# Even frequencies through both transforms first, batch 1's scans behind them

## The chip, the cores and the metric

The kernel runs on one core of a Trainium2 chip. The metric is device time of one execution in microseconds. Three runs of the kernel before gave 487.95, 489.83 and 489.97 us; the median is 489.83 us. The engines are named as the profile names them: PE (TensorE, matmul), DVE (VectorE), ACT (ScalarE), POOL (GpSimd) and SP (SyncE, whose queue issues most transfers here).

## The reference

Three blocks run one after the other on a batch of 2, 768 tokens and 8 heads of 48 (so 384 model columns):

```python
# 1. attention with a decaying state, per batch and head
y[t] = r[t] @ (state + (u * k[t])[:, None] * v[t])      # u: the token's own term
state = w[t][:, None] * state + k[t][:, None] * v[t]
# 2. Fourier mixing over tokens and columns, then a wide layer
mixed = real(fft(fft(x, axis=1), axis=2)); u = x + mixed
un = (u - mean(u)) / sqrt(var(u) + 1e-6)                # over the 384 columns
x = u + relu(un @ w_ch1) @ w_ch2                        # 384 -> 1536 -> 384
# 3. gated layer with a spatial product over the 768 tokens
h = gelu_tanh(x @ w_in); a, v = h[..., :512], h[..., 512:]
out = x + (a * (w_sg @ (norm(v) * g) + b_sg)) @ w_out
```

## The kernel before, in words

**Attention** (`attention`, line 345) goes by head pairs: n = 0 to 3 are the pairs of batch 0, n = 4 to 7 those of batch 1. Tokens stand in 6 chunks of 128. `prep` (line 191) loads the pair's decays `wx`, its r and k (`rk`) and v, and on DVE makes the running product of the decays (L224, "the scan"), then L236, L240 and L241 scale r and k by it; ACT does logarithm and exponential (L229, L230), POOL one product (L238). PE then multiplies scores (`sc_ps`, L281), transposes k (`kn_ps`, L295), makes chunk states (`kv_ps`, L304; chained by a scan on DVE, L310; copied by ACT, L312) and values (`y_ps`, L324 and L333). L335 adds the token's own term, L340 and L341 sum and subtract token halves, and ACT (L342) and POOL or DVE (L343) write the result as a high and a low part, `AH` and `AL`. The tiles P, rk, prk, XE, XO are the places of decays and r, k; pairs 1, 2 and 3 use `prk`, `XE` and `XO`.

**The own term** (`own_term`, line 249) has two forms. For the pairs in the set `TM` (4 to 7 before) `prep` loads r, k and u in token order (`in_ruk`, L215), and it is two elementwise products (L255 on DVE or POOL by the set `PV`, L257 on POOL) and a sum on DVE (L258). For the others DVE multiplies r and k (L234) and PE sums over head columns with six matmuls (`dg_ps`, L264), which ACT copies (L265). Either way POOL multiplies the sum by v (L270).

**The Fourier step** (`fourier`, line 451) has `frequencies` (the transform over tokens for one third j of the columns, on PE into `x_ps`, high part by ACT L400 and low part by DVE L401), `own_tokens` (PE brings x itself into the right layout, `t_ps`, copied by ACT L420 into `uT`) and `mixed` (the transform over columns, `d_ps`, added to `uT` by DVE, L440 to L449). Frequencies with even and odd index (e = 0 and 1) are apart: e = 0 gives the first half of the columns of `uT`, e = 1 the second.

**The wide layer** (`moe1`, line 460) goes over four halves of 384 tokens: (batch 0, e = 0), (batch 0, e = 1), and the same of batch 1. Each half is centred (`centre`: the mean by matmuls `mu`, then `uc`, L488; `split_centred`: `us`, L494 and L495), then for 12 blocks f of hidden columns PE makes `z_ps` (9 matmuls), ACT the high part (L518), DVE the low part `z_lo` (L519), and PE `ch` (9 matmuls, one block behind). Every weight block is read as 8-byte words and turned into a high and low part: three operations on DVE (L162 to L164, into the one buffer `st`), one on ACT (L168), one on POOL (L169).

**Order.** The code is written as generators that are stepped in turn, and a scheduler then orders each engine's queue; every queue runs in that order. Before, attention of batch 1 is stepped beside the Fourier step of batch 0 (`merge` with `F0`, line 884), and the rest of it, with batch 1's Fourier step, beside the wide layer (`merge(first(), second(), FR)`, line 914). A second set of rules are order-only dependencies (`behind`). The last stage (`gating`) follows when the wide layer is done; the change does not touch it.

Of the kernel before, what the change touches and what calls it, by code (L numbers as in the profile page):

```python
# [20 lines left out]

FR = 0.7
CFG1 = dict(v=2, dv=2, dg=2, sc=4, yt=2)
CFGF = dict(ps=2, su=2)
F0 = 1.0
KC = 9
LA = 6
KV = range(1)
NJ0 = 28
JP = -1000000  # L30
LNPE = ((0, 0), (0, 1))
GF = 4
STB = 1
TB = 1
XB = 1
LEAD = 0
PV = range(4)
TM = range(4, 8)
YB = 1
# [7 lines left out]
C = 128  # L47
# [48 lines left out]
def fused(ctx, tc, ins, out, dbg=None):  # L96
# [94 lines left out]
    def prep(n, b, p, ap):  # L191
# [6 lines left out]
        v = m1.tile([C, NC_ * 2 * D], F32, name="v", tag=("us_hi", "us_lo")[p - 2]) if b == 0 and p >= 2 else ap([C, NC_ * 2 * D], "v")  # L198
        if b == 0 and p < 3:
            prod, y0 = (x[:PR, p * S:(p + 1) * S].rearrange("p (c t) -> p c t", c=NC_) for x in spare)  # L200
        else:
            prod = ap([C, ROW], "prod") if n in TM else ap([PR, NC_, C], "prod")
            y0 = ap([PR, NC_, C], "y0")

# [11 lines left out]
        for c0, c1 in parts:  # L216
# [9 lines left out]
            if b:  # L226
                behind(scan, summed[min(n - 2, NP - 1)])
            Pi = P[:, cs, 1:C + 1]
# [162 lines left out]

    def frequencies(b, AB, X, j):

        for e in range(2):
            nx = NCOS[e] + NSIN
            x_ps = ps(b, [C, 512], "x_ps", XB)[:, :nx]
            for c in range(3):
                mm3(x_ps, AB[:, 3 * e + c, j * C:(j + 1) * C], tdft[:, e, c, :nx], c == 0, c == 2)
            x = X[e][j][:, :nx]
            nc.scalar.copy(x.hi, x_ps)  # L400
            nc.vector.tensor_tensor(out=x.lo, in0=x_ps, in1=x.hi.bitcast(F32), op=ALU.subtract)  # L401
            yield
# [20 lines left out]
    def mixed(b, ap, X, uT, e):  # L423
# [18 lines left out]
        for f, (d, s) in enumerate(us):  # L442
            for g, x, y in ((0, d, s),) if f == 0 else ((1, d, s), (2, s, d)):
                ut = uT[:, g, e * HT:(e + 1) * HT]

                to, x = ut[:, :HT // 2 + 1 - e], x[:, :HT // 2 + 1 - e]
                nc.vector.tensor_tensor(out=to, in0=to, in1=x, op=ALU.add)
                to, y = ut[:, HT // 2 + 1 - e:][:, ::-1], y[:, 1 - e:HT // 2]
                nc.vector.tensor_tensor(out=to, in0=to, in1=y, op=ALU.add)  # L449

    def fourier(b, ap, back, AB, X, uT, js):
        for j in js:
            yield from frequencies(b, AB, X, j)
        yield from own_tokens(b, back, AB, uT)
        for e in range(2):
            mixed(b, ap, X, uT, e)
            yield


    def moe1(mp, halves, uT, w1, w2):  # L460
# [69 lines left out]

        ucs = centre(*halves[0])
        last = None
        for n, (b, h) in enumerate(halves):
            us = split_centred(ucs)
            sq = ucs[0]
# [293 lines left out]
    with ExitStack() as main, ExitStack() as low, ExitStack() as late, ExitStack() as att:  # L829
# [26 lines left out]
        def through(b, p):  # L856

            if b == 0 and p > 0:
# [200 lines left out]
```

## Time and profile before

| | us |
|---|---|
| median of three runs | 489.83 |
| the profiled execution | 486.78 |
| its span, first to last instruction | 485.0 |
| PE busy / DVE / ACT / POOL in the span | 433.7 / 269.1 / 173.1 / 177.1 |

The span is what the views below divide; the profiled execution lasts 1.8 us longer than its span and 3.05 us less than the median of the runs. "Busy" counts the time in which an engine has an instruction under way; PE's matmuls overlap each other, so their durations add up to more than their busy time. PEclk is the clock that was granted to PE as a share of full speed, and 1.00 is full speed. In the timeline a row reads: start, duration of the run of equal instructions, engine, line, operation, what it writes from what, shapes, count, and in brackets how long the engine had stood idle before it and what ended that.

### The profile page before, as it was taken

How to read it: one execution, taken by the hardware profiler on the slowest of the kernel's cores; microseconds unless marked ns; L12 is line 12 of the kernel's file. 1: busy time of each engine (PE TensorE's matmuls, PEld its weight loads, DVE VectorE, ACT ScalarE, POOL GpSimd, SP SyncE). 2: the span in 40 equal slices, each digit the busy share in tenths (PEclk: the TensorE clock that was granted, in tenths of full speed). 3: DMA queues.
4: the chain of work that ended last, by engine and by line, in shares of the span. 5: the costliest groups of instructions: out<-in, count | busy, mean ns of one | idle time of the engine just before them, and what ended most of it. 6: DMA issues, size and time to landing. Idle time of an engine off the chain costs nothing. (4 is left out here: it accounts for less than half of the span.)

```text
span 485.0 us, 6874 instructions
## 1 busy us (share of the span) xinstructions
PE 433.7 (89%) x2666; PEld 409.1 (84%) x2666; DVE 269.1 (55%) x453; ACT 173.1 (36%) x368; POOL 177.1 (37%) x179
## 2 busy tenths in 40 slices
PE   9569973896896968999999799999999999999995
PEld 9468863885796957999999599999988998999994
DVE  5983259967697686463137961452148734811332
ACT  3534453552452433443323531431355403311110
POOL 2864366754466463320003540110356524200330
PEclk9869997698997987999999999999999999999998
DMA  8983504341644311040000310000243200010002
GB/s 209 266 303 82 164 1 148 118 133 55 257 146 132 106 38 33 1 131 0 1 0 2 109 55 0 1 0 1 65 115 84 64 1 2 33 66 1 0 18 88
DMA packets 14074, 36.75 MB, mean 76 GB/s; under 512 B 1808, under 2 KB 5680, under 8 KB 13648
## 3 DMA queue, kind: packets, MB, share of 16 engines
q1 hardware_dynamic: 13456, 32.54, 22.3%
q0 software_dynamic: 576, 3.68, 2.2%
q8 instruction: 23, 0.38, 0.3%
q14 instruction: 19, 0.16, 0.1%
HBM read 33.86 MB, written 2.36 MB: 75 GB/s over the span
## 5 line engine op out<-in xcount | busy, mean ns | idle before, releaser
L109 PE MATMUL ch<-z_hi,w 128*128 128x384 f32 x288 | 82.1, 343 | 5.7 <-ACT z_hi L518 2.9
L109 PE MATMUL z_ps<-us_hi,w 128*128 128x384 f32 x288 | 83.1, 351 | 1.4 <-ACT us_hi L494 1.4
L519 DVE SCALAR_TENSOR_TENSOR z_lo<-z_ps,z_hi 128x384 fp32r<-128x384 f32 x48 | 26.5, 553 | 68.9 <-ACT z_hi L518 68.2
L109 PEld LDWEIGHTS ch<-z_hi,w 128*128 128x128 f32 x288 | 53.1, 191 | 8.2 <-ACT z_hi L518 4.4
L109 PEld LDWEIGHTS z_ps<-us_hi,w 128*128 128x128 f32 x288 | 54.3, 193 | 3.6 <-ACT us_hi L494 2.0
L109 PE MATMUL ch<-z_lo,w 128*128 128x384 f32 x144 | 50.3, 350 | 5.7 <-DVE z_lo L519 5.5
L109 PE MATMUL z_ps<-us_lo,w 128*128 128x384 f32 x144 | 49.6, 344 | 0.0
L518 ACT ACTIVATE z_hi<-z_ps 128x384 fp32r<-128x384 f32 x48 | 23.3, 489 | 55.0 <-PE z_ps L109 41.4
L285 POOL TENSOR_SCALAR_AFFINE_SELECT sc<-sc 128x384 f32<-128x384 f32 x32 | 23.9, 769 | 41.2 <-ACT sc L284 41.2
L608 POOL TENSOR_TENSOR vn_lo<-t_g,vn_hi 128x384 fp32r<-128x384 f32 x16 | 16.1, 1014 | 57.1 <-ACT vn_hi L607 57.1
L109 PEld LDWEIGHTS ch<-z_lo,w 128*128 128x128 f32 x144 | 27.8, 193 | 7.6 <-DVE z_lo L519 7.4
L604 DVE SCALAR_TENSOR_TENSOR t_g<-s_ps,g,bsg 128x384 f32<-128x384 f32 x16 | 9.6, 616 | 43.2 <-PE s_ps L109 43.0
L169 POOL TENSOR_TENSOR w<-st,w 128x384 fp32r<-128x384 f32 (+1 forms) x18 | 24.8, 1380 | 22.9 <-ACT w L168 22.8
L109 PE MATMUL s_ps<-wsg_hi,vn_lo 128*128 128x384 f32 x96 | 32.3, 336 | 0.0
L109 PE MATMUL s_ps<-wsg_hi,vn_hi 128*128 128x384 f32 x96 | 32.3, 336 | 0.0
L109 PE MATMUL s_ps<-wsg_lo,vn_hi 128*128 128x384 f32 x96 | 32.3, 336 | 0.0
L333 PE MATMUL y_ps<-v,sc 128*128 128x120 f32 (+1 forms) x192 | 31.6, 287 | 0.0
L109 PEld LDWEIGHTS z_ps<-us_lo,w 128*128 128x128 f32 x144 | 27.9, 194 | 0.1
L333 PEld LDWEIGHTS y_ps<-v,sc 128*128 128x128 f32 x192 | 26.7, 197 | 0.8 <-issue 0.5
L169 POOL TENSOR_TENSOR win_lo<-st,win_hi 128x384 fp32r<-128x384 f32 x8 | 8.3, 1053 | 48.8 <-ACT win_hi L168 48.8
L169 POOL TENSOR_TENSOR wsg_lo<-raw,wsg_hi 128x384 fp32r<-128x384 f32 x12 | 12.4, 1035 | 32.3 <-ACT wsg_hi L168 32.2
L109 PE MATMUL x_ps<-tdft,AH 128*128 128x386 f32 (+1 forms) x72 | 20.3, 374 | 4.2 <-ACT AH L342 4.2
(261 smaller groups left out, 1047.5 us busy)
## 6 DMA issues: line engine op xcount, KB each, us to landing
raw<-in_w SPq DMA_DIRECT2D x12, 384.0 KB, 3.9
w_raw<-in_w SPq DMA_DIRECT2D x12, 384.0 KB, 4.6
raw<-in_win SPq DMA_DIRECT2D x8, 384.0 KB, 3.6
prod<-in_ruk SPq DMA_DIRECT2D x4, 624.0 KB, 4.3
tdft<-in_tdft POOLq DMA_DIRECT2D x2, 1158.0 KB, 9.2
v<-in_v SPq DMA_DIRECT2D x8, 288.0 KB, 6.0
raw<-in_wsg SPq DMA_DIRECT2D x12, 192.0 KB, 2.4
out<-o SPq DMA_DIRECT2D x12, 192.0 KB, 1.9
```

Source lines behind the costliest of these rows:

```text
L109: nc.tensor.matmul(o, lhsT=x, rhs=y, start=start and i == 0, stop=stop and i == len(ps) - 1, **kw)
L169: nc.gpsimd.tensor_tensor(out=w.lo[to], in0=x, in1=w.hi[to].bitcast(F32), op=ALU.subtract)
L285: nc.gpsimd.affine_select(out=sc, in_=sc, pattern=[[0, 3], [1, C]], compare_op=ALU.is_gt, fill=0.0, base=0, channel_multiplier=-1)
L333: nc.tensor.matmul(y3[:, i, to], lhsT=sc[h][:, i, :], rhs=vf[:, of], start=c == 0, stop=True, skip_group_check=c > 0)
L518: nc.scalar.activation(out=z.hi, in_=z_ps, func=AF.Relu)
L519: nc.vector.scalar_tensor_tensor(out=z.lo, in0=z_ps, scalar=0.0, in1=z.hi.bitcast(F32), op0=ALU.max, op1=ALU.subtract)
L604: nc.vector.scalar_tensor_tensor(out=t, in0=s_ps[h], scalar=g[:, f:f + 1], in1=bsg[:, hs], op0=ALU.mult, op1=ALU.add)
L608: nc.gpsimd.tensor_tensor(out=vn.lo[:, f, 3 * h:3 * h + 3], in0=th, in1=vn.hi[:, f, 3 * h:3 * h + 3].bitcast(F32), op=ALU.subtract)
```

## The change

Four things change. The own terms of pairs 1, 2 and 3 take the elementwise form (`TM` from 1), so their `in_ruk` loads, 624 KB each, come between the first loads. Attention of batch 1 is no longer stepped beside batch 0's Fourier step; its scans stand behind the last addition of that step's even frequencies (`first_through`, order only). The Fourier step does e = 0 through `frequencies`, `own_tokens` and `mixed` before it does e = 1, and the first half is centred in between. The first two weight blocks are stepped earlier, four rather than six blocks are kept ahead (`GF`, `LA`), `FR` goes from 0.7 to 0.6, so each step of the wide layer takes 1.67 rather than 1.43 steps of batch 1 with it, and the second half's mean is made as the others (two additions on DVE, a split on ACT and POOL, two matmuls) instead of three matmuls in f32.

```diff
-FR = 0.7
+FR = 0.6
-F0 = 1.0
-LA = 6
+LA = 4
-LNPE = ((0, 0), (0, 1))
-GF = 4
+LNPE = ((0, 0),)
+GF = 2
-TM = range(4, 8)
+TM = range(1, 8)
...
             if b:
-                behind(scan, summed[min(n - 2, NP - 1)])
+                behind(scan, first_through)
...
-    def frequencies(b, AB, X, j):
-
-        for e in range(2):
+    def frequencies(b, AB, X, j, *es):
+
+        for e in es:
...
     def fourier(b, ap, back, AB, X, uT, js):
         for j in js:
-            yield from frequencies(b, AB, X, j)
+            yield from frequencies(b, AB, X, j, 0)
         yield from own_tokens(b, back, AB, uT)
-        for e in range(2):
-            mixed(b, ap, X, uT, e)
-            yield
+        end = mixed(b, ap, X, uT, 0)
+        yield end
+        for j in js:
+            yield from frequencies(b, AB, X, j, 1)
+        mixed(b, ap, X, uT, 1)
+        yield
...
         ucs = centre(*halves[0])
+        us = split_centred(ucs)
+        yield 0, -1
...
-        merge(fourier(0, f_room, ..., uT[0], (2,)), att_steps, F0, False, LEAD)
+        for got in fourier(0, f_room, ..., uT[0], (2,)):
+            if got:
+                first_through = got
+                mixing = moe1(m1, HALVES, uT, w1, w2)
+                next(mixing)
...
-        ahead(GF)
-        mixing = moe1(m1, HALVES, uT, w1, w2)
         merge(first(), second(), FR)
```

Where instructions stand now is shown at three places of DVE's queue. First the opening, where the pairs of batch 0 are prepared. Before (AH and prod take r times k, prk is pair 1, XE pair 2, XO pair 3):

```order
L234 TENSOR_TENSOR AH<-prk 112x768
L241 SCALAR_TENSOR_TENSOR rk<-AL,rk 112x384
L656 TENSOR_TENSOR unit<-unit 112x1
L236 SCALAR_TENSOR_TENSOR prk<-prk 112x768
L224 SCALAR_TENSOR_TENSOR XE<-XE,d_91 112x774
L234 TENSOR_TENSOR AH<-XE 112x768
L240 SCALAR_TENSOR_TENSOR AL,unit<-prk,AL 112x768
L236 SCALAR_TENSOR_TENSOR XE<-XE 112x768
L224 SCALAR_TENSOR_TENSOR XO<-XO,d_91 112x774
L241 SCALAR_TENSOR_TENSOR prk<-AL,prk 112x768
L310 SCALAR_TENSOR_TENSOR kn<-kn,dec 112x288
```

In the changed kernel, at the same place:

```order
L236 SCALAR_TENSOR_TENSOR prk<-prk 112x768
L241 SCALAR_TENSOR_TENSOR rk<-AL,rk 112x384
L662 TENSOR_TENSOR unit<-unit 112x1
L255 TENSOR_TENSOR AH<-AH 128x576
L224 SCALAR_TENSOR_TENSOR XE<-XE,d_91 112x774
L240 SCALAR_TENSOR_TENSOR AL,unit<-prk,AL 112x768
L241 SCALAR_TENSOR_TENSOR prk<-AL,prk 112x768
L236 SCALAR_TENSOR_TENSOR XE<-XE 112x768
L310 SCALAR_TENSOR_TENSOR kn<-kn,dec 112x288
L258 TENSOR_REDUCE dg<-AH 128x12
L224 SCALAR_TENSOR_TENSOR XO<-XO,d_91 112x774
```

L241 of pair 1 (`prk`) stood behind the scans of XE and XO and two products L234; now it stands behind the scan of XE and the product L255.

Next the end of batch 0's attention. Before, from the last subtraction (L341) to the low part of the last pair (L343, `AL`):

```order
L341 TENSOR_TENSOR kn<-dv 128x288
L224 SCALAR_TENSOR_TENSOR prk<-prk,d_91 112x774
L224 SCALAR_TENSOR_TENSOR P<-P,d_91 112x774
L236 SCALAR_TENSOR_TENSOR prk<-prk 112x768
L343 TENSOR_TENSOR AL<-kn,AH 128x6x96
```

In the changed kernel (L160 to L162 are the three weight operations, which were L162 to L164; L335 is the last of pair 3):

```order
L160 TENSOR_SCALAR st<-raw 128x384 x2
L161 SCALAR_TENSOR_TENSOR st<-raw,st 128x384
L401 TENSOR_TENSOR XE<-x_ps,XE 128x386
L161 SCALAR_TENSOR_TENSOR st<-raw,st 128x384
L162 SCALAR_TENSOR_TENSOR st<-raw,st 128x384
L335 TENSOR_TENSOR dv<-y_ps,dv 128x288
L162 SCALAR_TENSOR_TENSOR st<-raw,st 128x384
L340 TENSOR_TENSOR kn<-dv 128x288
L341 TENSOR_TENSOR kn<-dv 128x288
L258 TENSOR_REDUCE dg<-prod 128x12
L343 TENSOR_TENSOR AL<-kn,AH 128x6x96
```

The two scans and L236 of batch 1 are gone from in front of `AL`; a weight block's operations and an own-term sum of batch 1 (L258) stand there.

Last, the start of the wide layer. Before, with the last additions of batch 0's Fourier step (`uT`) between the centred columns (`uc`, `us_lo`) and the first `z_lo` soon after:

```order
L488 SCALAR_TENSOR_TENSOR uc<-mu,uT_84 128x384
L449 TENSOR_TENSOR uT_84<-uT_84,su 128x192
L447 TENSOR_TENSOR uT_84<-uT_84,su 128x192
L488 SCALAR_TENSOR_TENSOR uc<-mu,uT_84 128x384 x2
L495 TENSOR_TENSOR us_lo<-uc,us_hi 128x384 x3
L162 TENSOR_SCALAR st<-w_raw 128x768
L163 SCALAR_TENSOR_TENSOR st<-w_raw,st 128x768
L519 SCALAR_TENSOR_TENSOR z_lo<-z_ps,z_hi 128x384
```

In the changed kernel, from the additions of the even frequencies on (`uc`, L492, was L488; `us_lo`, L499, was L495; P and prk are now pairs 4 and 5):

```order
L449 TENSOR_TENSOR uT_84<-uT_84,d_ps 128x191
L224 SCALAR_TENSOR_TENSOR P<-P,d_91 112x774
L224 SCALAR_TENSOR_TENSOR prk<-prk,d_91 112x774
L449 TENSOR_TENSOR uT_84<-uT_84,su 128x191
L447 TENSOR_TENSOR uT_84<-uT_84,su 128x193
L236 SCALAR_TENSOR_TENSOR rk<-rk,P 112x768
L258 TENSOR_REDUCE dg<-prod 128x12
L236 SCALAR_TENSOR_TENSOR prk<-prk 112x768
L440 SCALAR_TENSOR_TENSOR su<-ps,d_ps 128x192
L447 TENSOR_TENSOR uT_84<-uT_84,d_ps 128x192
```

Three rows further on DVE, the centred columns and what stands between them and the first `z_lo`:

```order
L449 TENSOR_TENSOR uT_84<-uT_84,d_ps 128x192
L492 SCALAR_TENSOR_TENSOR uc<-mu,uT_84 128x384 x3
L449 TENSOR_TENSOR uT_84<-uT_84,su 128x192
L240 SCALAR_TENSOR_TENSOR y_945,unit<-P,y_945 112x768
L499 TENSOR_TENSOR us_lo<-uc,us_hi 128x384 x3
L241 SCALAR_TENSOR_TENSOR rk<-y_945,rk 112x768
L224 SCALAR_TENSOR_TENSOR P<-P,d_91 112x774
L488 TENSOR_TENSOR uc<-uT_84 128x384
L489 TENSOR_TENSOR uc<-uc,uT_84 128x384
L160 TENSOR_SCALAR st<-w_raw 128x768
L161 SCALAR_TENSOR_TENSOR st<-w_raw,st 128x768
L523 SCALAR_TENSOR_TENSOR z_lo<-z_ps,z_hi 128x384 x2
```

Two additions of the even frequencies, and `uc`, stand behind the first two scans of batch 1, and the first `z_lo` (L523, which was L519) behind another scan, two operations of pair 4 and two additions.

## Rows read from the trace of the kernel before

**Rows 1.** Busy time by engine in four stretches; PEclk, DMA share, GB/s last.
```profile
core 0: us, PE busy (x) PEld busy (x) DVE busy (x) ACT busy (x) POOL busy (x), PEclk, DMA share, GB/s
0.00:74.00 74.00, 60.59 (x472) 55.52 (x472) 44.86 (x56) 32.19 (x70) 40.69 (x50) 0.91 0.59 168
74.00:120.00 46.00, 31.84 (x199) 27.83 (x197) 38.80 (x64) 19.91 (x48) 26.93 (x21) 0.81 0.36 118
120.00:207.00 87.00, 74.86 (x490) 67.53 (x491) 60.89 (x86) 34.73 (x71) 43.08 (x34) 0.90 0.31 100
207.00:480.00 273.00, 266.40 (x1509) 258.19 (x1507) 124.50 (x250) 86.23 (x179) 66.44 (x74) 1.00 0.12 36
```

**Rows 2.** PE's timeline at six places; the bracket says what it waited for.
```profile
27.95 1.65 PE L281 MATMUL sc_ps<-prk 48*128 48x128 f32 x12 [5.38 <-DVE prk L241]
...
73.51 0.63 PE L333 MATMUL y_ps<-v,sc 128*128 128x96 f32 x4
76.11 0.94 PE L281 MATMUL sc_ps<-rk 48*128 48x128 f32 x12 [1.97 <-DVE rk L241]
...
86.56 0.69 PE L109 MATMUL x_ps<-tdft,AL 128*128 128x386 f32 x1 [4.98 <-DVE AL L343]
...
101.81 0.63 PE L333 MATMUL y_ps<-v,sc 128*128 128x120 f32 x4
...
120.01 0.45 PE L109 MATMUL z_ps<-us_hi,w 128*128 128x384 f32 x1 [1.39 <-ACT us_hi L494]
```

**Rows 3.** PE's waits from 120 to 285 us: total, times, longest.
```profile
PE ch L109 <- DVE z_lo L519: 5.5, 3, 3.0
```

**Rows 4.** DVE's timeline in the opening.
```profile
23.66 2.08 DVE L224 TENSOR_TENSOR_SCAN XO<-XO,d 112x774 f32<-112x774 f32 x1
25.66 2.23 DVE L241 SCALAR_TENSOR_TENSOR prk<-AL,prk 112x768 f32<-112x768 f32 x1
...
33.62 0.96 DVE L241 SCALAR_TENSOR_TENSOR XE<-AL,XE 112x768 f32<-112x768 f32 x1
```

**Rows 5.** Transfers: issues, KB each, us from issue to landing.
```profile
prk<-in_rk SPq DMA_DIRECT2D x3, 672.0 KB, 5.3
...
XO<-in_wx SPq DMA_DIRECT2D x1, 338.6 KB, 12.6
```

**Rows 6.** The own term by matmuls: groups of PE up to 120 us.
```profile
L264 PE MATMUL dg_ps<-uh,AH 112*128 112x128 f32 x36 | 7.0, 346 | 0.0
...
L264 PE MATMUL dg_ps<-uh,prod 112*128 112x128 f32 x12 | 1.6, 282 | 0.0
```

**Rows 7.** The own term by products: groups of DVE and POOL, whole span.
```profile
L258 DVE TENSOR_REDUCE dg<-prod 128x12 f32<-128x576 f32 x4 | 3.0, 744 | 2.8 <-POOL prod L257 2.8
...
L257 POOL TENSOR_TENSOR prod<-prod 128x576 f32<-128x576 f32 x4 | 7.2, 1792 | 0.2
...
L255 POOL TENSOR_TENSOR prod<-prod 128x576 f32<-128x576 f32 x4 | 5.9, 1482 | 5.2 <-DMA prod<-in_ruk 5.2
```

**Rows 8.** POOL's timeline while DVE ran pair 1's L241.
```profile
24.09 2.99 POOL L238 TENSOR_TENSOR XE<-XE,AL 112x768 f32<-112x768 f32 x1
```

**Rows 9.** DVE's timeline beside batch 0's Fourier step.
```profile
72.57 2.15 DVE L240 SCALAR_TENSOR_TENSOR y<-P,y 112x768 f32<-112x768 f32 x1 [0.54 <-POOL rk L238]
...
80.88 2.94 DVE L224 TENSOR_TENSOR_SCAN P<-P,d 112x774 f32<-112x774 f32 x1
83.74 2.09 DVE L236 SCALAR_TENSOR_TENSOR prk<-prk 112x768 f32<-112x768 f32 x1
...
105.25 0.45 DVE L335 TENSOR_TENSOR dv<-y_ps,dv 128x288 f32<-128x288 f32 x1
```

**Rows 10.** The second half's mean on PE.
```profile
193.16 2.11 PE L482 MATMUL mu<-uT,ones_r 128*128 128x384 f32 x6
```

**Rows 11.** POOL's part of a weight block's conversion, whole span, larger form.
```profile
L169 POOL TENSOR_TENSOR w<-st,w 128x768 fp32r<-128x768 f32 x6 | 11.8, 1970 | 10.9 <-ACT w L168 10.8
```

**Rows 12.** SP's queue: the last pair's decays are asked for.
```profile
164.38 0.33 SPq L207 DMA_DIRECT2D prk<-in_wx  x1
```

More of the change, by code (lines that the diff above doesn't have):

```diff
@@ L35 @@
 XB = 1
-LEAD = 0
 PV = range(4)
-TM = range(4, 8)
+TM = range(1, 8)
 YB = 1
@@ L198, in prep @@
         v = m1.tile([C, NC_ * 2 * D], F32, name="v", tag=("us_hi", "us_lo")[p - 2]) if b == 0 and p >= 2 else ap([C, NC_ * 2 * D], "v")
-        if b == 0 and p < 3:
-            prod, y0 = (x[:PR, p * S:(p + 1) * S].rearrange("p (c t) -> p c t", c=NC_) for x in spare)
-        else:
-            prod = ap([C, ROW], "prod") if n in TM else ap([PR, NC_, C], "prod")
-            y0 = ap([PR, NC_, C], "y0")
+        y0 = spare[1][:PR, p * S:(p + 1) * S].rearrange("p (c t) -> p c t", c=NC_) if b == 0 and p < 3 else ap([PR, NC_, C], "y0")
+        if n not in TM:
+            prod = ap([PR, NC_, C], "prod")
+        elif b == 0 and p < 3:
+            prod = spare[0][:, :ROW] if p == 1 else f_room([C, ROW], "prod")
+        else:
+            prod = ap([C, ROW], "prod")
         parts = ((0, 3), (3, 6)) if n == 0 else ((0, 6),)
@@ L448, in mixed @@
                 to, y = ut[:, HT // 2 + 1 - e:][:, ::-1], y[:, 1 - e:HT // 2]
-                nc.vector.tensor_tensor(out=to, in0=to, in1=y, op=ALU.add)
+                end = nc.vector.tensor_tensor(out=to, in0=to, in1=y, op=ALU.add)
+        return end
     def fourier(b, ap, back, AB, X, uT, js):
         for j in js:
-            yield from frequencies(b, AB, X, j)
+            yield from frequencies(b, AB, X, j, 0)
         yield from own_tokens(b, back, AB, uT)
-        for e in range(2):
-            mixed(b, ap, X, uT, e)
-            yield
+        end = mixed(b, ap, X, uT, 0)
[4 more added lines that the diff above has]
+        yield
     def moe1(mp, halves, uT, w1, w2):
@@ L531, in moe1 @@
         ucs = centre(*halves[0])
+        us = split_centred(ucs)
+        yield 0, -1
         last = None
         for n, (b, h) in enumerate(halves):
-            us = split_centred(ucs)
+            us = split_centred(ucs) if n else us
             sq = ucs[0]
@@ L864, in through @@
                 if p < NP - 1:
-                    run(frequencies(0, made(0), X0, p - 1))
+                    run(frequencies(0, made(0), X0, p - 1, 0, 1))
+                if p == 2:
+                    ahead(GF)
         done = 0
@@ L878, in fused @@
         spare = a_room([C, 3 * S], "AH"), a_room([C, 3 * S], "AL")
+        first_through = None
         att_steps = attention(a_room, made, through)
@@ L883, in fused @@
         back = [m1.tile([C, NC_, C], F32R, name=f"back_{x}", tag=f"us_{x}") for x in ("hi", "lo")]
-        merge(fourier(0, f_room, [(t[:, 0:3], t[:, 3:6]) for t in back], made(0), X0, uT[0], (2,)), att_steps, F0, False, LEAD)
+        for got in fourier(0, f_room, [(t[:, 0:3], t[:, 3:6]) for t in back], made(0), X0, uT[0], (2,)):
+            if got:
+                first_through = got
+                mixing = moe1(m1, HALVES, uT, w1, w2)
+                next(mixing)
         dump("u0", uT[0])
```

## The prediction

> **What bounds the kernel now.** I read the busy times by stretch first [rows 1]: the reader sees that PE is all but full from 207 us on (266.4 of 273 us), so little in the last 278 us can get shorter by a new order; the time to be won lies ahead of 207 us, where PE has work for 60.6 of 74, 31.8 of 46 and 74.9 of 87 us, and that at a mean granted clock of 0.91, 0.81 and 0.90 of full speed. Then PE's timeline, for what ends its idle time [rows 2]: in the opening it stands 5.38 us for pair 1's L241 on DVE, in the middle 4.98 us for the low part `AL` of batch 0's last pair, also on DVE, and after 120.01 us, where the wide layer begins, it waits in several small pieces, of which the `z_lo` of DVE is the largest named [rows 3]. So ahead of 207 us the end is set by DVE's queue: what stands in front of the instruction that PE wants. DVE is busy for 38.8 of the 46 us up to 120 us and for 60.9 of the 87 us behind it [rows 1].
>
> **The opening, batch 0's attention.** PE's wait for pair 1 ends at 27.95 us [rows 2], behind an L241 that DVE began at 25.66 us, after the scan of XO, 2.08 us [rows 4]. In the new order that scan, the L236 of XE and two products L234 stand behind it, and one L255 of 576 columns in front: the scan alone is 2.1 us, three more operations of 768 columns at the 0.96 us of an undisturbed L241 [rows 4] are 2.9, and L255 costs about 0.8 of that back: 4.2 us to win. Against it: two `in_ruk` loads, 624 KB each, go ahead of XO's decays. Those decays took 12.6 us from issue to landing [rows 5] in a stretch that moves 168 GB/s on average [rows 1]; at that rate each load takes 3.7 us, so XE's arrive up to 3.7 us later and XO's 7.4. If DVE stands for all of the first, 0.5 us is left; if for none, 4.2. I take 4, since the trace has no wait for these decays. The own terms: 36 of the 48 matmuls `dg_ps` go; all 48 are 8.6 us of overlapping durations [rows 6], so at three quarters 6.5; a part lay in that wait, the rest in a stretch in which PE had little idle time, so between 0 and 5; I take 2.5. What comes in their place, per pair L255, L257 and L258 of 1.5, 1.8 and 0.7 us [rows 7], is mostly POOL's, which is free for 33 of the first 74 us, and costs nothing as long as POOL reaches L270 before the values do; without that cover it is 2.5 us for each of pairs 2 and 3. Batch 0's last `y_ps`, at 74.1 us [rows 2], should come at 67.6.
>
> One rule of the Trainium skill speaks against this part. The row first: pair 1's L241 took 2.23 us while POOL ran an L238 of 2.99 us, and the L241 of XE 0.96 us [rows 4, 8]. The page "SBUF — State Buffer", section "Who interferes with whom", says that a Vector instruction with two inputs in SBUF contends with a GpSimd instruction that reads SBUF, and that the later one waits the other out. The row agrees. By it each added product on POOL could hold DVE once, at the row's 1.3 us; three of them at worst would make the opening's gain 3.9 us smaller, and the prediction below 484.4 in place of 480.5.
>
> **From there to the wide layer.** Before, from that last `y_ps` to `AL` it is 12.4 us (74.1 to 86.5) [rows 2]: two scans and an L236 of batch 1 stand in front, 7 us (the scan of 2.94 and the L236 of 2.09 us [rows 9], and one more scan at the 2.08 us of the opening's [rows 4]). Now L335, L340, L341 and L343 remain, about 2 us, behind a weight block and an L258 which wait for POOL (two own-term products at 1.5 and 1.8 us, one after a 624 KB load). POOL becomes the late one: I take 7.5 us, `AL` at 75 us, with 3 and 13 as ends. Before, from `AL` to the first `z_ps` it is 33.5 us. Of e = 1 only its first transform is partly out of the way, and the new queue puts two scans, two L236 and an L258 between the even additions and `uc`: 2.9, 2.1 and 0.7 us for the dearest of each [rows 7, 9]. Gone from that stretch are batch 1's matmuls and most of its products on DVE. I take 28 us, between 23 and 34: the wide layer starts at 103 us where it was 120, a gain of 17.
>
> **What is handed on.** PE now has, behind that start, what it did of pair 4 ahead of it: its scores, transposes, chunk states and first values, from 76.11 to 101.81 us [rows 2], 11 rows that add up to 7.4 us and overlap a little: 6.9. The second half's mean gives back 2.11 us [rows 10] less two matmuls of the same width: 1.5. DVE gets 7 operations of batch 1 that it had done before 120 us, the first and last in [rows 9], 10.4 us, and two additions, 1.1.
>
> So the stretch that was 87 us has 74.9 + 6.9 − 1.5 = 80.3 us for PE and 60.9 + 11.5 = 72.4 for DVE. If PE keeps its share (86%), it lasts 93.3 us; if DVE keeps its own (70%), 103.4; if PE never waited, 80.3. The first `z_lo` now stands behind a scan and two operations of pair 4, 4 to 6 us where the trace has 5.5 us in all [rows 3], so a little over the first: 94.7 us. The stretch ends at 103 + 94.7 = 197.7 us against 207. `GF` and `LA` I cost at nothing: in the new queue each weight block still stands three to four `z_lo` ahead of its use, and the cover is PE's eighteen matmuls per block; gone, PE waits for a conversion's last leg, POOL's 2.0 us [rows 11], and the DVE and ACT work ahead of it. Behind 207 us the order differs little and PE is full.
>
> The sum: −17 + 6.9 − 1.5 + 2.3 (94.7 less 87 + 5.4) = −9.3 us on the profiled execution of 486.8: 477.5. That execution was 3.05 us (0.6%) under the median of the runs, so against the median of 489.83 I predict 480.5 us.
>
> **Rivals.** (a) DVE keeps its share: the stretch takes 103.4 us and ends at 206.4. For it: both scans and the conversions are on DVE, which was already what PE waited for. Against it: DVE's 26 idle us in that stretch were waits for others. Time: 480.5 + 8.7 = 489.2.
> (b) PE finds work at all times: 80.3 us, nearly all the idle time goes; more realistically 84. For it: more independent matmuls lie side by side. Against it: even the best stretch before 207 us had PE at 86%. Time: 480.5 − 10.7 = 470.
> (c) Slower: the last two pairs of batch 1 come late. Their loads reuse the tiles of pairs 4 and 5 and are asked for only when those pairs' values are done, as at 164.38 us before [rows 12]; these values now come later against the wide layer, while DVE's queue has the scan and L236 of pairs 6 and 7 in front of a `z_lo`. If DVE reaches them before the data, it stands for a load, and with it PE, which has but one block in hand: 5.3 us of load [rows 5] and some 2 us of chain, the next scan, so 7, at two places. Against it: in the trace DVE had enough other work to reach these operations when the data was there. It decides where DVE gets to pair 6's L236 over 5 us before its r and k land. Time: 480.5 + 14 = 494.5.
> (d) The change does not do what it says: two of the even additions stand behind the scans in DVE's queue, so centring is not between the Fourier halves. That costs 4 to 5 us of the 17 and is in my 28 us; if the two scans and the two L236 behind them each met a product on POOL at the 1.3 us of [rows 4], 5 more: 485.5.
>
> **How the numbers follow.** Forecast 480.5, with its own range 474 to 486: 0.45. (a) 0.18, (b) 0.14, (c) 0.12, (d) 0.11. Within 0.5%, what a measurement of this kernel can just tell from no change, is 487.4 to 492.3. Faster: forecast, (b), (d) and a little of (a): 0.73; the same: most of (a), 0.14; slower: (c) and the end of (a), 0.13. The range from 469 to 491 takes in (a), (b) and (d) and leaves out (c).
>
> **What would show it.** In the new profile: pair 1's `sc_ps` at 24 us; batch 0's last `y_ps` near 67.6; `AL` near 75, with POOL's L257 as what ends the wait; the first `z_ps` near 103; the first `ch` waiting 4 to 6 us for `z_lo`; batch 1's last values near 196 to 200 us, two to three blocks further into the second half than before. It would be wrong if the first `z_ps` came after 110 us, or if DVE were busy for over 85% between there and batch 1's last values with PE waiting for `z_lo` throughout.

## The result, and the profile after

The changed kernel takes 482.6 us (median of 4 runs, 482.27 to 483.55) where the kernel before takes 489.9 us beside it (487.95 to 490.82): ratio 0.9859, 95% interval 0.9826 to 0.9893. Forecast were 480.5 us and a range of 469 to 491. The profiled execution took 482.27 us, span 480.6, against 486.78 and 485.0. The number was nearly right. The reasons behind it were mostly wrong, which takes the rest of this document to show.

First the busy times by stretch, the answer to [rows 1], with the same columns:

```profile
0.00:74.00 74.00, 59.17 (x430) 53.83 (x431) 50.12 (x64) 30.70 (x65) 42.74 (x55) 0.84 0.74 211
74.00:120.00 46.00, 31.95 (x161) 28.26 (x159) 36.96 (x60) 19.14 (x45) 24.58 (x18) 0.70 0.37 123
120.00:207.00 87.00, 77.61 (x557) 70.85 (x556) 58.01 (x92) 40.64 (x82) 48.15 (x39) 0.96 0.26 83
207.00:480.00 273.00, 263.45 (x1484) 256.00 (x1482) 121.44 (x245) 83.27 (x174) 64.93 (x73) 0.98 0.13 37
```

The reader is to look at PE (first number behind the length) and at the granted clock (0.84, 0.70, 0.96, 0.98). Up to 120 us PE is busy for 91.1 us, hardly less than the 92.4 before, but at a lower clock; between 120 and 207 us it is busier and faster than before. Whether the opening, to which I had given 6.5 of the 17 us, got shorter is read from single rows.

PE's timeline at the places of [rows 2] (start, length, what it waited for in brackets):

```profile
24.02 1.65 PE L281 MATMUL sc_ps<-prk 48*128 48x128 f32 x12 [3.85 <-DVE prk L241]
...
51.15 1.42 PE L107 MATMUL x_ps<-tdft,AH 128*128 128x386 f32 x4 [2.15 <-ACT AH L342]
...
72.57 0.46 PE L324 MATMUL y_ps<-U,XO 112*128 112x96 f32 x2 [1.08 <-DVE dv L335]
...
74.21 0.63 PE L333 MATMUL y_ps<-v,sc 128*128 128x96 f32 x4
81.11 1.01 PE L107 MATMUL x_ps<-tdft,AH 128*128 128x386 f32 x2 [6.27 <-ACT AH L342]
...
83.26 0.69 PE L107 MATMUL x_ps<-tdft,AL 128*128 128x386 f32 x1 [0.71 <-DVE AL L343]
...
111.09 1.01 PE L107 MATMUL z_ps<-us_hi,w 128*128 128x384 f32 x2 [1.98 <-ACT us_hi L498]
...
122.94 0.55 PE L107 MATMUL ch<-z_lo,w 128*128 128x384 f32 x1 [2.68 <-DVE z_lo L523]
...
127.22 0.34 PE L476 MATMUL var<-z_hi,ones_r 128*128 128x384 f32 x1
```

Pair 1's scores come at 24.02 us, 3.9 earlier, as forecast. But batch 0's last `y_ps` ends at 74.84 where it ended at 74.14, `AL` is at 82.3 (85.8 before), and the first `z_ps` at 111.1 (120.0 before, 103 forecast). So the opening got no shorter. By my own sign the reasoning was wrong, whatever the time: I had set 110 us as the latest start of the wide layer. DVE's timeline in the same stretch says what stood in the way:

```profile
17.72 3.94 DVE L224 TENSOR_TENSOR_SCAN XE<-XE,d 112x774 f32<-112x774 f32 x1
...
66.31 1.41 DVE L160 TENSOR_SCALAR st<-raw 128x384 uint32<-128x384 uint32 x1 [2.41 <-DMA raw<-in_w]
...
72.07 0.45 DVE L335 TENSOR_TENSOR dv<-y_ps,dv 128x288 f32<-128x288 f32 x1
...
77.49 0.45 DVE L335 TENSOR_TENSOR dv<-y_ps,dv 128x288 f32<-128x288 f32 x1
...
78.70 1.65 DVE L341 TENSOR_TENSOR kn<-dv 128x288 f32<-128x288 f32 x1
81.64 0.75 DVE L258 TENSOR_REDUCE dg<-prod 128x12 f32<-128x576 f32 x1 [1.30 <-POOL prod L257]
82.31 0.89 DVE L343 TENSOR_TENSOR AL<-kn,AH 128x576 fp32r<-128x576 f32 x1
```

The first weight block's conversion (L160) waits 2.41 us for its load, and the values of pair 3 (L335) stand behind it; the last L335 stands behind the second block until 77.49, 2.65 us after its `y_ps` was done.

One marker is used from here on: the matmul `var` (L476 after), which each half of the wide layer makes with its second block. It is the same place in the wide layer of every kernel, though not in batch 1's work beside it, and from the third half's `var` to the end all of them take 203.4 to 204.5 us. So the end is decided ahead of it. Each profile is one execution, up to some 3 us off the median of its kernel, so a difference of two marks is no surer than that. Starts of three marks in PE's timeline of each profiled execution, us:

| kernel | first `z_ps` | first half's `var` | third half's `var` | span |
|---|---|---|---|---|
| before | 120.0 | 130.1 | 281.5 | 485.0 |
| changed | 111.1 | 127.2 | 277.2 | 480.6 |
| before, new constants | 120.8 | 131.1 | 277.7 | 482.2 |
| changed, old constants | 111.3 | 126.9 | 281.7 | 485.2 |
| changed, FR 0.7 | 113.2 | 129.3 | 281.8 | 485.4 |
| changed, FR 0.5 | 110.9 | 127.1 | 284.6 | 488.4 |
| changed, weights behind the attention | 110.4 | 128.4 | 286.2 | 489.8 |
| changed, scans early | 117.0 | 126.1 | 278.4 | 481.9 |
| changed, own terms by matmuls | 112.1 | 129.9 | 278.1 | 482.1 |

Before, the way from the first `z_ps` to `var` takes 10.1 us, after 16.1. Of the 8.9 us that the wide layer starts earlier, 2.9 are left two blocks later. The two ways as stretches, before and after; the reader is to look at the granted clock, third from the end (1.00 and 0.63):

```profile
120.00:130.10 10.10, 8.08 (x49) 7.12 (x50) 6.43 (x10) 5.16 (x11) 4.00 (x5) 1.00 0.88 312
```

```profile
111.10:127.20 16.10, 11.73 (x36) 10.39 (x37) 13.84 (x21) 7.03 (x13) 7.69 (x5) 0.63 0.63 218
```

### The profile page after: what moved, and what is told of

It reads as the page before. It is cut to its first block, busy times and chain, and to the rows that moved or that the text cites. A ratio compares the mean times of both kernels' runs of the same rounds, so it can differ in the third digit from the quotient of the medians.

```text
span 480.6 us, 6825 instructions
## 1 busy us (share of the span) xinstructions
PE 432.2 (90%) x2626; PEld 408.9 (85%) x2626; DVE 266.5 (55%) x458; ACT 173.8 (36%) x366; POOL 180.4 (38%) x183
## 5 line engine op out<-in xcount | busy, mean ns | idle before, releaser
L107 PE MATMUL ch<-z_hi,w 128*128 128x384 f32 x288 | 85.3, 358 | 2.8 <-ACT z_hi L522 1.5
L523 DVE SCALAR_TENSOR_TENSOR z_lo<-z_ps,z_hi 128x384 fp32r<-128x384 f32 x48 | 26.4, 553 | 64.4 <-ACT z_hi L522 64.2
L107 PEld LDWEIGHTS ch<-z_hi,w 128*128 128x128 f32 x288 | 55.9, 201 | 5.1 <-ACT z_hi L522 2.9
L107 PE MATMUL ch<-z_lo,w 128*128 128x384 f32 x144 | 51.5, 358 | 5.3 <-DVE z_lo L523 5.3
L614 POOL TENSOR_TENSOR vn_lo<-t_g,vn_hi 128x384 fp32r<-128x384 f32 x16 | 16.1, 1014 | 57.2 <-ACT vn_hi L613 57.2
L475 POOL TENSOR_TENSOR z_lo<-uc,z_hi 128x384 fp32r<-128x384 f32 x7 | 9.5, 1363 | 67.5 <-ACT z_hi L474 67.4
L107 PEld LDWEIGHTS ch<-z_lo,w 128*128 128x128 f32 x144 | 29.0, 201 | 6.7 <-DVE z_lo L523 6.7
L333 PE MATMUL y_ps<-v,sc 128*128 128x120 f32 (+1 forms) x192 | 34.5, 304 | 0.0
L285 POOL TENSOR_SCALAR_AFFINE_SELECT sc<-sc 128x384 f32<-128x384 f32 x32 | 24.5, 780 | 19.5 <-ACT sc L284 19.3
L333 PEld LDWEIGHTS y_ps<-v,sc 128*128 128x128 f32 x192 | 29.4, 213 | 1.2 <-issue 0.3
```

Source lines behind the costliest of these rows:

```text
L107: nc.tensor.matmul(o, lhsT=x, rhs=y, start=start and i == 0, stop=stop and i == len(ps) - 1, **kw)
L285: nc.gpsimd.affine_select(out=sc, in_=sc, pattern=[[0, 3], [1, C]], compare_op=ALU.is_gt, fill=0.0, base=0, channel_multiplier=-1)
L333: nc.tensor.matmul(y3[:, i, to], lhsT=sc[h][:, i, :], rhs=vf[:, of], start=c == 0, stop=True, skip_group_check=c > 0)
L475: nc.gpsimd.tensor_tensor(out=parts.lo, in0=x, in1=parts.hi.bitcast(F32), op=ALU.subtract)
L523: nc.vector.scalar_tensor_tensor(out=z.lo, in0=z_ps, scalar=0.0, in1=z.hi.bitcast(F32), op0=ALU.max, op1=ALU.subtract)
L614: nc.gpsimd.tensor_tensor(out=vn.lo[:, f, 3 * h:3 * h + 3], in0=th, in1=vn.hi[:, f, 3 * h:3 * h + 3].bitcast(F32), op=ALU.subtract)
```

## Experiments

Each run was timed in five rounds beside the kernel before, on the same chip; ratios are to that kernel. Its median was 489.9 us beside the changed kernel and 488.2 to 489.2 us beside the others, so where a difference in us and one of ratios disagree by a microsecond, the ratios are the safer.

**1. The weight blocks' place in the changed kernel.** My first theory was that the conversions in front of L335 had eaten the opening's gain.

```diff
-                if p == 2:
-                    ahead(GF)
...
         for got in att_steps:
             if got == 0:
                 break
+        ahead(GF)
```

> The changed kernel with its first two weight blocks asked for behind batch 0's attention (as late as the old place as far as DVE's queue goes), and nothing else. Theory Q (queue): in the changed kernel the conversion of these blocks (L160 to L162) stands in DVE's queue in front of batch 0's last L335, L340 and L341, and its loads stand in SP's in front of pair 5's in_ruk. Then PE's wait of 1.08 us at 72.57 goes, the last y_ps of batch 0 ends near 73.5 instead of 74.8, AL begins near 77 instead of 82.3, the first z_ps near 107 instead of 111.1, some of the gain being paid back by conversions that now stand nearer to it; time 478.5 to 480. Rival N (no cause): the conversions are as much in the way later, DVE being full from 98 to 111 us, so the first z_ps stays within 1.5 us of 111 and the time within 1 us of 482.6.

Measured: 491.36 us, ratio 1.0041 (1.001 to 1.0072), 8.8 us slower than the changed kernel. Neither theory's time came; rival N has the first `z_ps` right (within 1.5 us of 111). DVE's and then PE's timeline:

```profile
79.15 0.76 DVE L343 TENSOR_TENSOR AL<-kn,AH 128x576 fp32r<-128x576 f32 x1 [0.74 <-ACT AH L342]
...
101.49 2.16 DVE L161 SCALAR_TENSOR_TENSOR st<-raw,st 128x384 uint32<-128x384 uint32 x1
...
109.26 1.47 DVE L492 SCALAR_TENSOR_TENSOR uc<-mu,uT 128x384 f32<-128x384 f32 x3
...
161.54 5.04 DVE L240 SCALAR_TENSOR_TENSOR y<-P,y 112x768 f32<-112x768 f32 x1 [1.72 <-POOL rk L238]
```

```profile
110.40 1.01 PE L107 MATMUL z_ps<-us_hi,w 128*128 128x384 f32 x2 [7.22 <-ACT us_hi L498]
...
197.58 1.66 PE L281 MATMUL sc_ps<-prk 48*128 48x128 f32 x12 [5.18 <-issue]
```

`AL` did come 3.2 us earlier, but the conversions then stood in front of `uc`, and PE lost the gain in one wait of 7.22 us. From the first half's `var` to the third's it then takes 7.8 us more: pair 6's L240 takes 5.04 us (2.84 in the changed kernel), and pair 7's scores come at 197.58 instead of 190.45. So the early blocks do delay the opening, and are still worth 9 us behind it.

**2. The same place in the kernel before.** In `through`, batch 0's pair 2, and nothing else:

```diff
                     run(frequencies(0, made(0), X0, p - 1))
+                if p == 2:
+                    ahead(2)
```

> The kernel before with one thing of the change alone: its first two weight blocks asked for at batch 0's pair 2. Theory W (weights are the gain): asked for behind the attention the changed kernel took 491.4 us, so their place is worth 9 us there, and in the kernel before the four blocks' conversions stood on DVE from 86.4 to 115 us, right where it sets the end; moved into the opening, where DVE is free for 18 of 40 us, they give most of the change's 7 us by themselves: 482 to 485. Rival K (works only with the rest): with batch 1's scans ahead of AL, DVE is as full from 66 to 90 us as behind, conversions and scans push each other, AL comes 3 to 5 us later and the gain is under 2.5 us: 486.5 to 490.

Measured: 487.62 us, ratio 0.999 (0.9959 to 1.002): no change, as rival K has it. Alone the place is worth nothing; it is a condition of the new order, not the gain.

**3. Weight blocks still earlier.** Two at pair 1, two at pair 2:

```diff
-                if p == 2:
-                    ahead(GF)
+                if p < 3:
+                    ahead(2 * p)
```

> The changed kernel with two weight blocks asked for at batch 0's pair 1 and two more at pair 2, in place of two at pair 2. Theory W: what a block converted in the opening saves behind it goes on; blocks 0 and 1 no longer stand in front of pair 3's first L335 (PE's 1.08 us at 72.57), the others are done before the transforms: the first z_ps comes at 107 to 109, the time is 478 to 480.5. Rival O (opening pays): the loads stand in SP's queue in front of pair 5's and 6's decays and in_ruk and four more conversions stand in front of batch 0's last L335 and L341; AL comes 3 us later than 82.3, the first z_ps at 111 to 114, 482 to 485.

Measured: 483.2 us, ratio 0.9895 (0.9861 to 0.9929). Theory W's 478 to 480.5 did not come; the first `z_ps` is at 112.3 us, within rival O. From the changed kernel it can't be told apart.

**4. Own terms of pairs 1 to 3 by matmuls again.**

```diff
-TM = range(1, 8)
+TM = range(4, 8)
```

> The changed kernel with the own terms of batch 0's pairs 1 to 3 by matmuls again (TM = 4 to 7). Prediction's step: these 36 matmuls cost PE 2.5 us of the opening, so the last y_ps of batch 0 comes 2.5 us later and the time goes to about 485. Rival F (filling): from 41 us on PE waits in the opening for DVE and ACT (1.00, 2.15, 2.27 us at 42.74, 51.15, 64.66), so matmuls there fill idle time and keep the granted clock from falling (it was 0.5 from 51.2 to 54.9 us and from 64.7 to 68.5 us), while POOL and DVE lose three products and a reduction each: the last y_ps comes at 74 to 75 us as now or earlier, and the time is 481 to 483.

Measured: 484.5 us, ratio 0.9908 (0.9876 to 0.994). Two rows of PE, and one of DVE:

```profile
51.10 1.22 PE L107 MATMUL x_ps<-tdft,AH 128*128 128x386 f32 x4
...
72.79 0.63 PE L333 MATMUL y_ps<-v,sc 128*128 128x96 f32 x4
```

```profile
70.65 0.45 DVE L335 TENSOR_TENSOR dv<-y_ps,dv 128x288 f32<-128x288 f32 x1
```

With 36 matmuls more, the first transform starts at the same 51.1 us, now without the wait of 2.15 us, and the last `y_ps` comes 1.4 us earlier, not 2.5 later. The matmuls had filled time in which PE waits anyway: in this rival F is right. They did not keep the clock up, as rival F also has it: from 51.2 to 54.9 us PE has 0.56 of full speed here and 0.54 in the changed kernel. These stretches, before, changed, and this run:

```profile
51.20:54.90 3.70, 3.62 (x33) 3.23 (x33) 1.28 (x3) 2.46 (x6) 2.03 (x3) 1.00 0.85 242
```

```profile
51.20:54.90 3.70, 3.70 (x17) 3.70 (x18) 0.00 (x0) 0.00 (x0) 2.75 (x2) 0.54 0.49 136
```

```profile
51.20:54.90 3.70, 3.70 (x18) 3.70 (x19) 0.00 (x0) 0.00 (x0) 2.49 (x3) 0.56 0.69 190
```

At 71.0 us PE is at the same place in both kernels (the last matmul of this transform starts at 71.03 and 71.15). The 1.4 us come after that, from DVE's queue: L335 starts at 70.65 instead of 72.07 us, one operation of the weight block earlier, and PE's wait of 1.08 us for it is gone. The whole is 1.9 us slower than the changed kernel, with intervals that overlap, and above rival F's 481 to 483; whether the products gain behind the opening stays open.

**5. Batch 1's scans early.**

```diff
-                behind(scan, first_through)
+                behind(scan, summed[min(n - 2, NP - 1)])
```

> The changed kernel with batch 1's scans behind the butterfly of two pairs before, as in the kernel before, instead of behind the first Fourier half's additions. Theory S (scans are the change): two scans and the L236 behind them, 7 us, stand again in front of AL, which goes from 82.3 to 87 or later; PE does pair 4's first part, 6.9 us, ahead of the wide layer again; the first z_ps comes near 117 and the time near 486. Rival M (only moved): the 4.7 us of scans and 2.9 us of L236 are missing between AL and the first z_ps instead, that stretch goes from 27.9 to about 21 us, the first z_ps comes at 109 to 111, PE has 6.9 us less to do behind it, and the time is 479 to 482.

Measured: 483.63 us, ratio 0.9883 (0.9843 to 0.9923), not told apart from the changed kernel. The first `z_ps` comes at 117.0 us as theory S says, not earlier as rival M has it, and the time is not S's 486: by `var`, at 126.1 us, the 6 us are made good. The start of the wide layer is no measure of the gain, because in the changed kernel the scan and two operations of pair 4 hold up the first `z_lo` instead.

**6. The old order of the Fourier steps.**

```diff
         for j in js:
-            yield from frequencies(b, AB, X, j, 0)
+            yield from frequencies(b, AB, X, j, 0, 1)
         yield from own_tokens(b, back, AB, uT)
         end = mixed(b, ap, X, uT, 0)
+        mixed(b, ap, X, uT, 1)
         yield end
-        for j in js:
-            yield from frequencies(b, AB, X, j, 1)
-        mixed(b, ap, X, uT, 1)
-        yield
```

> The changed kernel with batch 0's and batch 1's Fourier steps in the old order (both frequencies of the third part, then own tokens, then both mixings), the scans still behind the even additions. Theory E (even first pays): centring can begin only behind the odd additions, the first z_ps comes 3 to 5 us later, near 115, time 485 to 486. Rival D (the queue has it that way already): in the changed kernel DVE's queue has the odd sums ahead of uc anyway, so uc, the first z_ps and the time stay within 1 us: 481.6 to 483.6.

Measured: 482.67 us, ratio 0.9864 (0.9826 to 0.9902): rival D. The order of the even frequencies, the first half of what the change is named for, is worth nothing that can be measured; experiment 5 says the same of the second half, the place of the scans.

**7. Scans behind all the even additions.** `mixed` returns all its last additions, and each scan goes behind every one:

```diff
-                behind(scan, first_through)
+                for end in first_through:
+                    behind(scan, end)
```

> The changed kernel with batch 1's scans behind all four chains of even additions, where the changed kernel has two additions behind the scans. Prediction's rival (d) put 4 to 5 us on this. Theory P: the last even additions come at 100.9 instead of 105.3 us, PE's mu no longer waits 2.1 us, but uc needs the odd part's DVE work too, so that 2 to 4 of the 4.7 us of scans leave the chain in front of the first z_ps: z_ps at 107 to 109, and as the scans then stand in front of the us_lo or z_lo, a part is given back: 479.5 to 481.5. Rival Z: the start of the wide layer does not set the end (with the scans in front of AL it started at 117 and the time was 483.6), DVE's sum of work up to pair 7 does: first z_ps earlier, time within 1 us of 482.6.

Measured: 482.09 us, ratio 0.9881 (0.9853 to 0.9908): the time is rival Z's. The first `z_ps`, at 112.0 us, is not earlier, which neither theory had; `var` is at 126.6.

**8. The old constants in the changed kernel.** Of the structural edits taken back one by one only the weight blocks' place mattered, and that is a condition of the new order (experiment 2). The stepping of batch 1 beside the Fourier step (`F0`) was not taken back alone. That left the constants.

```diff
-FR = 0.6
-LA = 4
-LNPE = ((0, 0),)
-GF = 2
+FR = 0.7
+LA = 6
+LNPE = ((0, 0), (0, 1))
+GF = 4
```

> The changed kernel with the old constants: FR 0.7, LA 6, GF 4 and the mean of both of batch 0's halves on PE. Prediction: the constants cost nothing but the second half's mean, 1.5 us of PE: 483 to 484.5. Rival L: with LA 6 two more blocks stand in DVE's queue in front of each z_lo and the scan of pair 6 comes later in the order (FR 0.7): 486 or more.

Measured: 486.93 us, ratio 0.9971 (0.9944 to 0.9999), 4.3 us slower than the changed kernel: most of the gain is gone. The number is rival L's; its reason, `LA`, was not tried alone. Pair 7's scores come at 203.3 us instead of 190.4.

**9. The new constants in the kernel before.** The same four lines the other way.

> The kernel before with the four new constants (FR 0.6, LA 4, GF 2, one mean on PE) and nothing else of the change. Theory R: the constants bring pair 6's and 7's scans forward by one z_lo each in the old order too, pair 7's sc_ps from 197.8 to about 194, and the mean's 1.5 us go: 484.5 to 487. Rival J (only jointly): in the kernel before pair 7 was not what came last, with its scan already seven z_lo behind the start; the constants are worth less than 1.5 us there and the change's 7 us need both: 487 to 490.

Measured: 483.89 us, ratio 0.9897 (0.9866 to 0.9927): the constants alone bring the larger part of the change, which is theory R, and a little more than it has. From the changed kernel (0.9859) this run can't be told apart. The mark that the expectation takes, 197.8 us, is the second part of pair 7's scores; it comes at 189.0, the first part at 179.0 instead of 182.4, so further forward than expected.

Experiments 8 and 9 with the two kernels make a square:

| | old constants | new constants |
|---|---|---|
| old structure | 1 | 0.9897 (0.9866 to 0.9927) |
| new structure | 0.9971 (0.9944 to 0.9999) | 0.9859 (0.9826 to 0.9893) |

The constants give 1.03% in the old structure and 1.12% in the new, some 5 us; the whole structure gives 0.29% and 0.38%, some 1.4 to 1.9 us, about the size of the intervals, so that it is hardly shown to be there at all. One constant is not quite the same in both rows: in the new structure `GF` also says how many weight blocks are converted in the opening. The same square in the profiles, from the first half's `var` to the third's (length, busy PE, ..., granted clock third from the end). Before; before with the new constants; changed with the old constants; changed:

```profile
130.10:281.50 151.40, 136.93 (x863) 128.40 (x862) 95.30 (x164) 57.76 (x124) 52.31 (x42) 0.94 0.19 58
```

```profile
131.10:277.70 146.60, 134.20 (x858) 126.14 (x858) 97.88 (x167) 58.16 (x127) 53.76 (x45) 0.95 0.24 73
```

```profile
126.90:281.70 154.80, 142.78 (x940) 132.64 (x940) 89.88 (x158) 62.20 (x135) 50.81 (x43) 0.96 0.14 41
```

```profile
127.20:277.20 150.00, 140.31 (x937) 132.17 (x936) 89.02 (x163) 62.72 (x138) 56.67 (x46) 0.97 0.18 53
```

The constants shorten this stretch by 4.8 us in either structure. The structure makes it 3.4 us longer in either (77 and 79 matmuls more, the work of pair 4 that it hands on) and brings `var` 3.2 and 3.9 us forward: it breaks about even.

**10. FR alone.**

```diff
-FR = 0.6
+FR = 0.7
```

> The changed kernel with FR 0.7 instead of 0.6 and nothing else: batch 1's pairs 6 and 7 stand one and two z_lo later in DVE's queue. With all four old constants the time was 486.9, pair 6's sc_ps came at 172.6 instead of 166.7 and pair 7's at 203.3 instead of 190.4, while LA and GF leave DVE's queue as it is. Theory R (rate): the total follows the time at which batch 1's last pair is through, since from there PE is full; FR alone brings pair 7's sc_ps to 197 or later and the time to 484.5 to 487. Rival U (mean): the second half's mean on PE, 1.5 us, and its place ahead of pair 7 is the larger part of the 4.3 us; FR alone gives 482 to 484.

Measured: 486.06 us, ratio 0.9949 (0.9916 to 0.9982): 3.5 us slower, so FR carries most of what the constants give in the new structure (0.90% of 1.12%), as theory R says. DVE's, POOL's, PE's timeline and two stretches:

```profile
164.94 5.05 DVE L240 SCALAR_TENSOR_TENSOR y<-P,y 112x768 f32<-112x768 f32 x1 [1.74 <-POOL rk L238]
169.93 0.55 DVE L523 SCALAR_TENSOR_TENSOR z_lo<-z_ps,z_hi 128x384 fp32r<-128x384 f32 x1
```

```profile
164.87 1.85 POOL L167 TENSOR_TENSOR w<-st,w 128x768 fp32r<-128x768 f32 x1
166.68 1.40 POOL L343 TENSOR_TENSOR AL<-kn,AH 128x576 fp32r<-128x576 f32 x1
168.03 1.15 POOL L270 TENSOR_TENSOR dv<-v,dg 128x576 f32<-128x576 f32 x1
```

```profile
170.53 0.69 PE L107 MATMUL ch<-z_lo,w 128*128 128x384 f32 x1 [3.88 <-DVE z_lo L523]
```

```profile
170.00:176.00 6.00, 5.47 (x21) 5.03 (x23) 5.00 (x11) 1.78 (x4) 2.25 (x4) 0.50 0.15 39
...
204.00:210.00 6.00, 5.61 (x29) 5.11 (x31) 0.57 (x2) 1.08 (x3) 0.68 (x2) 0.50 0.01 3
```

Pair 6's L240 now starts just behind a POOL operation and lasts 5.05 us, as long as POOL has three in a row; a `z_lo` stands behind it, PE stands for 3.88 us and then works 6 us at 1.2 GHz, and once more from 204 us, when pair 7's scores have come late. In the changed kernel the same L240 takes 2.84 us, beside three shorter POOL operations (0.51, 1.15 and 0.51 us), and PE works at half speed for a shorter while behind it, and not at all where pair 7 comes (DVE's row, PE's row behind it, then four stretches):

```profile
161.28 2.84 DVE L240 SCALAR_TENSOR_TENSOR y<-P,y 112x768 f32<-112x768 f32 x1 [1.27 <-POOL rk L238]
```

```profile
166.71 0.95 PE L281 MATMUL sc_ps<-rk 48*128 48x128 f32 x12 [2.98 <-DVE rk L241]
```

```profile
164.00:168.00 4.00, 1.29 (x14) 1.16 (x15) 3.96 (x8) 0.26 (x1) 1.83 (x1) 0.94 0.00 0
168.00:172.00 4.00, 4.00 (x26) 3.70 (x24) 1.89 (x5) 2.11 (x6) 3.71 (x4) 0.64 0.37 97
186.00:190.00 4.00, 2.35 (x13) 2.02 (x13) 2.58 (x5) 1.20 (x3) 3.05 (x3) 1.00 0.00 0
190.00:196.00 6.00, 4.82 (x45) 3.98 (x44) 4.55 (x13) 2.91 (x8) 2.92 (x4) 1.00 0.00 0
```

Compared by sums from the first to the third `var`, FR 0.7 has 143.5 us of busy PE for 140.3 and 9.0 us of idle time for 9.7: all it loses there, 2.5 us, is clock. (In this one execution 2.1 us more are lost ahead of the first `var`, in work that FR does not pace.)

The L240 alone makes the difference look larger than it is: in the changed kernel the L241 behind it is drawn out too (2.48 us for an undisturbed 0.94), and PE stands 2.98 us for that one, only 0.9 less than the 3.88. What differs more is the work at half speed behind the wait. All this is read from one execution of each kernel, and it is not what the constants do in the old structure: there pair 6's L236 and L240 take 3.1 us together with the old constants and 5.2 with the new, and the new are faster all the same. What they save there stays open.

**11. FR further down.**

```diff
-FR = 0.6
+FR = 0.5
```

> The changed kernel with FR 0.5 instead of 0.6: pairs 6 and 7 stand one z_lo earlier in DVE's queue. Theory R: the same step again, pair 7's sc_ps at 184 to 188 instead of 190.4, the time 479 to 481. Rival V (load): pair 6 is bound by its rk, which landed 0.76 us after DVE asked for it, and pair 7 by the tile of pair 5, so earlier places in the queue only make DVE, and the z_lo behind it, stand for them: 482 to 485.

Measured: 492.54 us, ratio 1.0088 (1.0056 to 1.012), 9.9 us slower. Rival V's direction, and far worse than it says. PE's timeline, two places here and one in the changed kernel, then two stretches:

```profile
161.87 0.69 PE L107 MATMUL ch<-z_lo,w 128*128 128x384 f32 x1 [3.38 <-DVE z_lo L523]
...
190.77 1.17 PE L281 MATMUL sc_ps<-prk 48*128 48x128 f32 x12 [4.07 <-DVE prk L241]
```

```profile
190.45 0.94 PE L281 MATMUL sc_ps<-prk 48*128 48x128 f32 x12
```

```profile
160.00:170.00 10.00, 8.13 (x33) 7.32 (x34) 4.64 (x9) 2.62 (x6) 3.58 (x4) 0.53 0.01 2
...
190.00:198.00 8.00, 7.02 (x39) 6.12 (x40) 2.62 (x7) 1.46 (x4) 1.00 (x2) 0.58 0.00 0
```

Asked for earlier, pair 7 came no earlier (190.77 us for 190.45): PE merely had less of the wide layer in front of it, and stood. At pair 6 DVE did wait for a load, 1.34 us for r and k, as rival V has it; at pair 7 it waited 1.99 us for POOL's L238 instead. Two long stretches near 1.2 GHz follow, one behind the wait of 3.38 us at pair 6 and one behind the 4.07 us at pair 7. Of the three values tried, FR 0.6 lies between two losses.

**12. FR 0.5 with the scans behind all even additions**, the edits of 7 and 11 together.

> The changed kernel with FR 0.5 and with batch 1's scans behind all four chains of even additions, the two edits that theory R and the run with the scans behind all additions (482.1) speak for. Theory R: 478.5 to 480.5. Rival V: no better than either alone, 482 to 484.

Measured: 490.78 us, ratio 1.0039 (1.0002 to 1.0075). Theory R falls as a rule for going on in one direction. No run beat the changed kernel by more than can be measured.

## Why the prediction was right in number and wrong in cause

- **The opening: wrong.** Pair 1 was right (24.02 us for 24). The step that failed is that the lead of 4 us and the 2.5 us of `dg_ps` would add up to a last `y_ps` at 67.6. The lead was 3.5 us at pair 1's last values (47.7 for 51.2 us), 2.6 at the first transform, which waits 2.15 us for `AH` where it did not wait before, 1.2 us at the next `kn_ps` (57.8 for 59.0), PE having run at 0.54 of full speed from 51.2 to 54.9 us where it had 1.00 before, and below nothing behind the weight block, which I had not put into the opening at all. I took work off an engine in a stretch where it waits for others, and the time became idle time: in experiment 4, with the matmuls back, PE is at the same place at 51 and at 71 us. The lower clock is not shown to come of that idle time, since experiment 4 has it too without the wait; why it fell stays open.
- **From there to the wide layer: right.** Last `y_ps` to `AL` took 8.4 us by the prediction's marks (7.5 taken; from the end at 74.84 to PE's first use of `AL` at 83.26), ended by POOL's L257 by way of L258, and `AL` to the first `z_ps` took 28 (83.2 to 111.1). Nearly all of the 8 us that are missing at the wide layer lie in the opening.
- **What is handed on: the right kind, wrongly used.** I put the earlier start into the sum at its full price. Of 8.9 us, 6 were lost in the first two blocks, at a mean clock of 0.63 and with 2.68 us for `z_lo` (I had said 4 to 6); experiment 5 started 6 us later and lost 1.0 us. Batch 1's last `y_ps` is read at 210.5 us, not at 196 to 200 (205.9 before).
- **The constants: the missing term.** `GF` and `LA` were put at nothing; `FR` had no sentence of its own, and the second half's mean had 1.5 us. The runs give the four together some 5 us (1.03 and 1.12%), of which FR alone has 0.90% in the new structure. How the rest is shared out, and what FR and the mean each bring in the old structure, was not tried. My reckoning went by PE's busy share alone (86%) and had no term for the clock: with FR 0.7 the share from `var` to `var` is even a little higher than in the changed kernel (143.5 of 152.5 us for 140.3 of 150.0), and the loss is in the clock.
- **The sum.** −9.3 us were forecast; the medians give −7.3 and the two profiled executions −4.5. That the number came near was luck: a structural gain some five times too large (7.8 us without the mean's 1.5, against 1.4 to 1.9) stood in for a constant that I had not priced.
- **Rivals.** (c) is there in small: pair 6's L236 waits 0.76 us for its r and k; with FR 0.5 and with late weights the loss lies where pairs 6 and 7 come. (d) is right in its mechanism, as experiment 6 shows, and worth nothing by experiment 7.
- **Contention.** The rule of the Trainium skill that the prediction weighed ("SBUF — State Buffer", section "Who interferes with whom") agrees with this trace: the scan of XE took 3.94 us beside POOL's L285 and L257 where the scan of XO took 2.08 before [rows 4], and the L341 of 78.70 us took 1.65 beside POOL's L255 for an undisturbed 0.45. I had used it for the opening and in (d), at 1.3 us each; the dearer place is pair 6's L240, at 2.84 us in the changed kernel and 5.05 us with FR 0.7.

## What to carry to other kernels

When a change carries tuned constants along with its idea, price the constants first, and measure the square: idea alone, constants alone. A milestone that comes earlier is worth only what is left of it at the next point where all engines meet; choose a mark behind which every version takes the same time (here 203.4 to 204.5 us) and count idle time and granted clock up to it. Work taken off an engine that waits there for others buys nothing.

## What the hardware showed that I had not expected

A DVE operation that takes 0.94 us undisturbed lasted 5.05 us, held up by three POOL operations back to back, not by one: it ended 0.8 us after the third (169.99 for 169.18), as in the run with late weights (166.58 for 165.77). With FR 0.5 it met one, ended 0.8 us after that one and took 1.90 us. And with FR 0.7 and 0.5 a PE gap of 3.4 to 4.1 us was followed by 6 to 10 us of work at 1.2 GHz. At half speed the 5.47 busy us behind the gap of 3.88 us cost some 2.7 us more, an estimate from those two rows, so that the wait cost nearly twice what its row says; with FR 0.7 the whole loss in the stretch was clock. The length of a gap does not tell alone: before the change PE stood 2.18 us ahead of 65.7 us and went on at 1.00, in the changed kernel it stood 2.27 us ahead of 64.7 us and went on at 0.55.
